# Plain float32 products for the first six head pairs of an attention and feed-forward kernel, with earlier weight loads and a fourth bank for scores

## The chip, the core and the metric

The kernel runs on one core of a Trainium2 chip. The core has a matrix engine (TensorE, PE in the profile; PEld is its loading of weights), three engines for elementwise work (VectorE or DVE, ScalarE or ACT, GpSimd or POOL) and an engine (SyncE or SP) that here issues every DMA. Each engine runs its own instructions in the order in which they were written and waits on semaphores for the others. Matrix products land in PSUM, eight banks of 512 float32 columns on 128 partitions; POOL does not touch PSUM in this kernel. The metric is the device time of one execution, in microseconds (us), the median of several runs.

## The reference

```python
# q, k, v: 8 batches x 12 heads x 448 x 64
q_n, k_n = rmsnorm(q, g_q), rmsnorm(k, g_k)
scores = (1 / np.sqrt(64)) * (q_n @ k_n.transpose(0, 1, 3, 2))
attn = softmax(scores)                   # along the last axis
x = (attn @ v)                           # to (8 * 448) x 768
h = x @ w_in                             # 768 x 2048
y = (h * np.cos(h)) @ w_out              # 2048 x 768
```

The feed-forward weights come in as float64.

## The kernel before

**Split products.** TensorE multiplies operands of type float32r. To keep precision every operand is split in two: a high part (a cast to float32r) and a low part (the float32 value minus the high one). A product A B is then three matmuls: high-high, high-low and low-high; low-low is left out.

**Tiling.** Two heads make a pair; there are 48 pairs, six for each of eight batches. A pair has seven score tiles of 128 queries by 448 keys: tiles 0 to 2 of one head, 4 to 6 of the other, and tile 3, which holds 64 queries of each. Tiles j and j+4 use the upper and lower 64 rows of TensorE side by side. For a pair u:

- `prepare(u)` loads q and k once in rows (tile `sd`) for their norms and once transposed (`qd`, `kd`). ACT squares, DVE sums, POOL takes the power -1/2; the key's factors go through DRAM (`rk_d`) and come back as a row over all partitions (`rkb`). `k_norm` and `q_scale` on POOL apply the factors in place; `k_high`, `q_high` on ACT and `k_low`, `q_low` on POOL split the results into `khi`, `kl`, `qhi`, `ql`. `v_load` fetches each head's v, and `v_high`, `v_low` on POOL split it into `vs`, with high and low parts side by side.
- `attend(u)` computes the scores into PSUM tiles `S` (ring of three banks). `rowmin` on DVE scales a tile in place and takes its minimum, `expo` on ACT makes the exponentials `P` and their sums `sm`. Then come four chunks of keys. In each, seven transposes (`transp`, L411) bring `P` into the tile `PT`, of which there is only one (two banks); in chunk 1 an eighth transpose (L413) turns the sums. `pt_high` on ACT copies both heads' halves of `PT` to `hi` (L418), `pt_low` on DVE subtracts (`lo`, L426; in the last chunk into 64 rows of an earlier `hi`, L428), and `av` on PE multiplies by `vs` into the tile `O` (L438). High and low parts of v stand side by side in the weights, so that `O` has 128 rows, of which `x_half` (ACT, L448) and `x_sum` (DVE, L453) add upper and lower half.
- `x_norm` and `x_split` make the operand `xs` of the first feed-forward layer, split too.

**The first layer** of a batch (`multiply`) is 16 tiles, each of 18 matmuls (three parts of six) into the bank `ph`; it runs mixed with the next batch's attention. The last batch's layer and the whole second layer (L552 to L554) follow when attention is over.

**Weights.** A tile of `w_in` is loaded as 64-bit words (`raw`) and decoded to float32 by four DVE steps (L211, L213, L215, L219) and one on ACT, then split by ACT and POOL. The first three tiles are begun at once, the others at a time that `WAHEAD` sets in the plan. `w_out` is decoded in the same way from batch 2 on and stored to DRAM.

**What sets the order.** All parts are handed to a planner (`Plan`): each with an engine, a cost, a due time, what it reads and writes, and for DMAs a time to land. It runs a list schedule: whenever an engine is free in the plan, it gets the ready part with the earliest due time. Rings of buffers (`RING`) are part of the dependencies. The sequence that results is written out as each engine's program, so a changed cost or dependency can change the whole order. The plan's times are the planner's own and not measured.

Of the kernel before, what the change touches and what calls it, by code (L numbers as in the profile page):

```python
# [10 lines left out]
F32 = mybir.dt.float32  # L11
# [115 lines left out]
def tile_attention_moe(  # L127
# [14 lines left out]
    NP = NU // B  # L142
    NQT = 7
    NVC = 5
    NSP = 0
    NCC = 6
    NFC = w_in.shape[0]
    NOC = 6
# [160 lines left out]

    def k_norm(u):  # L310
        kd = pair[u]["kd"]
        nc.gpsimd.tensor_tensor(kd, kd, pair[u].pop("rkb"), ALU.mult)

    def k_high(u):
        nc.scalar.copy(tl(u, "khi", [128, S], F32R), pair[u]["kd"])
# [7 lines left out]

    def q_scale(u):
        qd = pair[u]["qd"]
        nc.gpsimd.tensor_scalar(qd, qd, gsc, 0.0, op0=ALU.mult, op1=ALU.add)

    def q_high(u):
        nc.scalar.copy(tl(u, "qhi", [128, 512], F32R), pair[u]["qd"])
# [5 lines left out]
    def v_load(u, hh):  # L335
        nc.sync.dma_start(tl(u, f"vd{hh}", [128, NVC, D], F32, "vd"), v[u, :, hh * NVC : hh * NVC + NVC])

    def v_high(u, hh):
        if hh == 0:
            tl(u, "vs", [128, 2 * NVC, 2, D], F32R)  # L340
        vs = pair[u]["vs"][:, hh * NVC : hh * NVC + NVC]
        nc.gpsimd.tensor_scalar(vs[:, :, 0, :], pair[u][f"vd{hh}"], 1.0, 0.0, op0=ALU.mult, op1=ALU.add)
# [2 lines left out]
        vs = pair[u]["vs"][:, hh * NVC : hh * NVC + NVC]  # L345
        nc.gpsimd.tensor_tensor(vs[:, :, 1, :], pair[u].pop(f"vd{hh}"), vs.bitcast(F32)[:, :, 0, :], ALU.subtract)

    def spare(u, t):
        return t == 3 and u < NSP


    def score(u, j):
        d = pair[u]
        ops = (("qhi", "khi"), ("ql", "khi"), ("qhi", "kl"))
        if j == 0:
            tl(u, "sm", [128, 4, NQT], F32)
        tiles = (3,) if j == 3 else (j, j + 4)
        for t in tiles:
            pool, tag = (ps_h, "ph") if spare(u, t) else (ps_s, "S")
            d["S", t] = pool.tile([128, 512], F32, tag=tag, name=f"S{u}_{t}")  # L360
        for n, (a, c) in enumerate(ops):
            for t in tiles:
                p0, p1 = (0, 128) if t == 3 else (0, 64) if t < 3 else (64, 128)
                nc.tensor.matmul(  # L364
                    d["S", t][:, :S], d[a][p0:p1, j * 128 : j * 128 + 128], d[c][p0:p1, :],
                    start=(n == 0), stop=(n == 2),
                )

    def rowmin(u, t):
# [44 lines left out]

    def pt_high(u, kc, hh):
        d = pair[u]
        hi = d["hi", kc, hh] = apool.tile([128, S], F32R, tag="hi", name=f"hi{u}_{kc}_{hh}", bufs=RING["hi"])
        nc.scalar.copy(hi, pt[:, hh * S : hh * S + S])  # L418
# [11 lines left out]
    def av(u, kc, hh):  # L430
        d = pair[u]
        if kc == 0 and hh == 0:
            d["O"] = ps_o.tile([128, 2, 512], F32, tag="O", name=f"O{u}")
        O = d["O"][:, hh, :S]
        ops = (((0, "hi", 0), (0, "lo", 0)), ((1, "hi", 1), (1, "lo", 1)), ((3, "lo", 2),), ((2, "hi", 3), (4, "hi", 2)))
        for n, (c, what, kb) in enumerate(ops[kc]):
            st = d["vs"][:, hh * NVC + c].rearrange("p a d -> p (a d)")
            nc.tensor.matmul(O, st, d.pop((what, kb, hh)), start=(kc + n == 0), stop=(kc + n == 4))  # L438

    xf = {}  # L440
    xs = {}

    def x_half(u, hh):
        O = pair[u]["O"]
        if hh == 0:
            xf[u] = xpool.tile([128, S], F32, tag=f"xf{u % NP}", name=f"xf{u}")
        a, c = (0, 64) if hh == 0 else (64, 0)
        nc.scalar.copy(xf[u][a : a + 64], O[c : c + 64, hh, :S])  # L448

    def x_sum(u, hh):  # L450
# [121 lines left out]
    ISS, LAND = 0.45, 5.0  # L572
    PER0, PER = 16.0, 19.0
    SPLIT = 50.0
    WAHEAD = 50.0
    KTURN = 1

    def base(u):
# [34 lines left out]
    def prepare(u):  # L613
        D0 = base(u)
        sd, r, kd, khi, qd, qhi = ([(n, u)] for n in ("sd", "r", "kd", "khi", "qd", "qhi"))
        add(SP, ISS, D0 - 45, st_load, u, w=sd, land=6.5)
        add(SP, ISS, D0 - 36, k_load, u, w=kd, land=LAND)
        add(SP, ISS, D0 - 30, q_load, u, w=qd, land=LAND)
        add(ACT, 0.95, D0 - 40, st_square, u, w=sd)
        add(DVE, 1.08, D0 - 38, st_reduce, u, r=sd, w=r)  # L620
        add(DVE, 0.25, D0 - 37, st_mean, u, w=r)
        rq = [("rq", u)]
        if u:
            add(POOL, 2.6, D0 - 34, st_pow, u, 0, 14, w=r + rq)
        else:
            add(POOL, 1.5, D0 - 34, st_pow, u, 7, 14, w=r)
        add(SP, ISS, D0 - 30, st_store, u, r=r, w=[("rkd", u)], land=LAND if u else 3.6)
        add(SP, 2 * ISS, D0 - 26, rk_load, u, r=[("rkd", u)], w=[("rkb", u)], land=6.5 if u else 4.5)
        if not u:
            add(POOL, 1.5, D0 - 17, st_pow, u, 0, 7, r=r, w=rq)  # L630
        add(POOL, 1.22, D0 - 18, k_norm, u, r=[("rkb", u)], w=kd)
        add(ACT, 0.53, D0 - 14, k_high, u, r=kd, w=khi)
        add(POOL, 1.22, D0 - 12, k_low, u, r=kd + khi, w=[("kl", u)])
        add(DVE, 0.25, D0 - 10, st_negate, u, r=r + rq, w=[("nr", u)])
        add(POOL, 0.8, D0 - 16, q_scale, u, r=[("gsc", 0)] + ([] if u else r), w=qd)
        add(ACT, 0.6, D0 - 10, q_high, u, r=qd, w=qhi)
        add(POOL, 1.33, D0 - 8, q_low, u, r=qd + qhi, w=[("ql", u)])
        for hh in range(2):
            vd, vs = [("vd", 2 * u + hh)], [("vs", u, hh)]
            add(SP, ISS, D0 - 12 + 6 * hh, v_load, u, hh, w=vd, land=LAND)  # L640
            add(POOL, 0.56, D0 + 6 * hh, v_high, u, hh, r=vd + ([] if u else r), w=vs)
            add(POOL, 0.91, D0 + 2 + 6 * hh, v_low, u, hh, r=vd, w=vs)

    def attend(u):
# [3 lines left out]
        lead = 0.0 if u < NP else None  # L648
        for j in range(4):
            tiles = (3,) if j == 3 else (j, j + 4)  # L650
            keys = [("ph", u) if spare(u, t) else ("S", 7 * u + 2 * j + n - min(u, NSP)) for n, t in enumerate(tiles)]
            dj = D0 + step * j
            add(PE, 0.88 if j < 3 else 0.62, dj, score, u, j, lead=lead,
                r=[("qhi", u), ("ql", u), ("khi", u), ("kl", u)], w=keys)
            for t, key in zip(tiles, keys):
                add(DVE, 0.7, dj + 1, rowmin, u, t, r=[("nr", u)], w=[key, ("sm", u, 1, t)])
            for n, (t, key) in enumerate(zip(tiles, keys)):
                add(ACT, 0.94, dj + 2, expo, u, t, r=[key, ("sm", u, 1, t)],
                    w=[("P", 7 * u + 2 * j + n), ("sm", u, 2, t)])
# [156 lines left out]
```

## Time and profile before

| what | value |
|---|---|
| median of three runs, device time | 1561.55 us (1559.03 to 1561.74) |
| the profiled execution | 1562.97 us |
| its span, first to last instruction | 1560.9 us |
| mean granted TensorE clock | 0.986 of full |
| PE busy | 1468.3 us, 94%, 7680 matmuls |
| DVE busy | 1060.8 us, 68% |
| ACT busy | 884.4 us, 57% |
| POOL busy | 885.1 us, 57% |
| first score matmul | 24.09 us |
| last copy of `O` (`x_half` of pair 47) | begins at 1011.87 us |

A whole-span average mixes stages with different limits: the first batch's attention without any feed-forward work beside it, seven batches of attention with the first layer of the batch before mixed in, and the second layer alone. Read the profile by stages therefore. PE's busy time counts from the start of a matmul to its end, and matmuls overlap, so a busy PE may still be able to take more.

The page's second part shows the stages. Each digit is the busy share of a fortieth of the span (39 us) in tenths:

```profile
PE   2777998899999999999999999999999999999999
DVE  6677999877877777777776675432566566666561
PEclk9898999999999999999999999999999999999999
```

In the first four digits PE is not full, in the fifth to seventh DVE is at 9, then PE is.

### The profile page before, as it was taken

How to read it: one execution, taken by the hardware profiler on the slowest of the kernel's cores; microseconds unless marked ns; L12 is line 12 of the kernel's file. 1: busy time of each engine (PE TensorE's matmuls, PEld its weight loads, DVE VectorE, ACT ScalarE, POOL GpSimd, SP SyncE). 2: the span in 40 equal slices, each digit the busy share in tenths (PEclk: the TensorE clock that was granted, in tenths of full speed). 3: DMA queues.
4: the chain of work that ended last, by engine and by line, in shares of the span. 5: the costliest groups of instructions: out<-in, count | busy, mean ns of one | idle time of the engine just before them, and what ended most of it. 6: DMA issues, size and time to landing. Idle time of an engine off the chain costs nothing.

```text
span 1560.9 us, 22589 instructions
## 1 busy us (share of the span) xinstructions
PE 1468.3 (94%) x7680; PEld 1239.3 (79%) x7680; DVE 1060.8 (68%) x1915; ACT 884.4 (57%) x1786; POOL 885.1 (57%) x727
## 2 busy tenths in 40 slices
PE   2777998899999999999999999999999999999999
PEld 1544787788877788878787788889999999999998
DVE  6677999877877777777776675432566566666561
ACT  4675776777766766766676665442344344344341
POOL 7666788876766676675576463141454445444441
PEclk9898999999999999999999999999999999999999
DMA  5336653465555455545544432168133232232220
GB/s 169 115 105 200 199 164 96 123 191 179 178 154 157 144 174 160 160 144 153 162 135 148 127 126 72 48 234 307 48 94 97 69 95 95 71 95 95 71 71 36
DMA packets 118435, 205.26 MB, mean 131 GB/s; under 512 B 19680, under 2 KB 97840, under 8 KB 118320
## 3 DMA queue, kind: packets, MB, share of 16 engines
q1 hardware_dynamic: 118320, 203.82, 41.7%
q8 instruction: 60, 0.98, 0.3%
q14 instruction: 55, 0.45, 0.1%
HBM read 150.47 MB, written 53.30 MB: 131 GB/s over the span
## 4 chain that ended last, share of the span: by engine, by line
PE 73%; DVE 8%; ACT 2%; issue 2%; POOL 1%; DMA 1%; SPq 0%; ACTq 0%; POOLq 0%; DVEq 0%
PE y L554 10%; PE y L552 10%; PE y L553 10%; PE ph L481 8%; PE ph L482 7%; PE ph L483 7%; PE O L438 7%; PE PT L411 6%; PE S L364 6%; DVE lo L426 2%; ACT hi L418 1%; DVE S L371 1%; DVE xf L453 1%; DVE hi L428 1%; DVE wo L213 1%
## 5 line engine op out<-in xcount | busy, mean ns | idle before, releaser
L481 PE MATMUL ph<-xs,wi 128*128 128x448 f32 x768 | 299.7, 390 | 3.7 <-ACT he L493 3.5
L482 PE MATMUL ph<-xs,wi 128*128 128x448 f32 x768 | 283.3, 369 | 1.4 <-POOL xs L467 1.4
L483 PE MATMUL ph<-xs,wi 128*128 128x448 f32 x768 | 282.8, 368 | 1.5 <-POOL wi L234 1.5
L552 PE MATMUL y<-g,wo 128*128 128x448 f32 x768 | 282.1, 367 | 0.0
L553 PE MATMUL y<-g,wo 128*128 128x448 f32 x768 | 281.9, 367 | 0.0
L554 PE MATMUL y<-g,wo 128*128 128x448 f32 x768 | 281.9, 367 | 0.0
L384 ACT ACTIVATE P<-S,sm 128x448 f32<-128x448 f32 x336 | 214.2, 641 | 97.9 <-DVE S L371 87.1
L418 ACT CAST hi<-PT 128x448 fp32r<-128x448 f32 x384 | 188.6, 535 | 118.6 <-PE PT L411 57.9
L536 POOL TENSOR_TENSOR g<-r,g 128x896 fp32r<-128x896 f32 x64 | 139.9, 2186 | 189.5 <-ACT g L538 189.5
L371 DVE TENSOR_SCALAR_CACHE_REDUCE S<-S,nr 128x448 f32<-128x448 f32 x336 | 219.9, 683 | 30.4 <-PE S L364 26.0
L426 DVE TENSOR_TENSOR lo<-PT,hi 128x448 fp32r<-128x448 f32 x288 | 166.7, 617 | 91.2 <-ACT hi L418 90.4
L411 PE MATMUL PT<-ident,P 128*128 128x128 f32 x1344 | 186.9, 281 | 1.6 <-ACT P L384 1.6
L411 PEld LDWEIGHTS PT<-ident,P 128*128 128x128 f32 x1344 | 164.7, 145 | 18.5 <-issue 2.7
L481 PEld LDWEIGHTS ph<-xs,wi 128*128 128x128 f32 x768 | 145.3, 189 | 34.2 <-issue 11.8
L483 PEld LDWEIGHTS ph<-xs,wi 128*128 128x128 f32 x768 | 145.2, 189 | 14.7 <-POOL wi L234 1.8
L482 PEld LDWEIGHTS ph<-xs,wi 128*128 128x128 f32 x768 | 145.7, 190 | 12.7 <-POOL xs L467 3.3
L552 PEld LDWEIGHTS y<-g,wo 128*128 128x128 f32 x768 | 144.2, 188 | 13.8 <-ACT ye L562 0.2
L553 PEld LDWEIGHTS y<-g,wo 128*128 128x128 f32 x768 | 144.2, 188 | 13.3
L554 PEld LDWEIGHTS y<-g,wo 128*128 128x128 f32 x768 | 144.2, 188 | 13.3
L518 DVE TENSOR_TENSOR r<-hb,n 128x896 f32<-128x896 f32 x64 | 93.1, 1455 | 85.7 <-POOL g L536 81.8
L438 PE MATMUL O<-hi,vs 128*128 128x448 f32 x384 | 133.0, 395 | 18.3 <-DVE xf L453 10.2
L529 DVE TENSOR_TENSOR r<-r,hb 128x896 f32<-128x896 f32 x64 | 73.9, 1154 | 108.5 <-ACT r L525 108.5
(69 smaller groups left out, 2567.2 us busy)
## 6 DMA issues: line engine op xcount, KB each, us to landing
h_d<-he SPq DMA_DIRECT2D x128, 224.0 KB
hb<-h_d SPq DMA_DIRECT2D x64, 448.0 KB
sd<-sd SPq DMA_DIRECT2D x48, 448.0 KB
vd<-v SPq DMA_DIRECT2D x96, 160.0 KB
qd<-qT SPq DMA_DIRECT2D x48, 256.0 KB
raw<-w_in SPq DMA_DIRECT2D x16, 768.0 KB
rawo<-w_out SPq DMA_DIRECT2D x32, 384.0 KB
wo_d<-rawo SPq DMA_DIRECT2D x32, 384.0 KB
```

Source lines behind the costliest of these rows:

```text
L371: nc.vector.tensor_scalar(d["S", t][:, :S], d["S", t][:, :S], d["nr"][:, t : t + 1], None, op0=ALU.mult, op1=ALU.min, accum_out=d["sm"][:, ...
L384: nc.scalar.activation(tl(u, f"P{t}", [128, S], F32, "P"), d.pop(("S", t))[:, :S], AF.Exp, bias=sm[:, 1, t : t + 1], scale=-1.0, accum_out ...
L411: nc.tensor.transpose(pt[:, t * 128 : t * 128 + 128], src, ident)
L418: nc.scalar.copy(hi, pt[:, hh * S : hh * S + S])
L426: nc.vector.tensor_tensor(lo, src, hi.bitcast(F32), ALU.subtract)
L438: nc.tensor.matmul(O, st, d.pop((what, kb, hh)), start=(kc + n == 0), stop=(kc + n == 4))
L481: nc.tensor.matmul(ph[:, :S], whi, x2[:, 0, :], start=(cc == 0), stop=False)
L482: nc.tensor.matmul(ph[:, :S], whi, x2[:, 1, :], start=False, stop=False)
L483: nc.tensor.matmul(ph[:, :S], wlo, x2[:, 0, :], start=False, stop=(cc == NCC - 1))
L552: nc.tensor.matmul(y, whi, hi, start=(fc == 0), stop=False)
L553: nc.tensor.matmul(y, whi, lo, start=False, stop=False)
L554: nc.tensor.matmul(y, wlo, hi, start=False, stop=(fc == NFC - 1))
```

## The change

For the first six pairs (batch 0, `NS32` and `NA32` are 6) scores and P v are computed with plain float32 operands and one matmul where three split ones stood:

- `k_norm` and `q_scale` write their results straight into `khi` and `qhi`, as float32; the casts and the low parts of q and k go.
- `v_whole` loads both heads' v with one DMA straight into `vs`; the split of v goes. SP then waits for `vs` to be free (P v of the pair two before), where it waited for POOL.
- `pt_high` copies `PT` as float32, the first head's half on ACT and the second's on DVE; `pt_low` goes. `av` is one matmul per chunk and head into 64 rows of `O`, and `x_sum` goes.
- `place` gives every fourth score tile of these pairs the bank `ph`, ahead of its first use by the first layer.
- `WAHEAD` goes from 50 to 100, which lets the loads of weights 3 and up start earlier in the plan.

```diff
     def k_norm(u):
         kd = pair[u]["kd"]
-        nc.gpsimd.tensor_tensor(kd, kd, pair[u].pop("rkb"), ALU.mult)
+        k = tl(u, "khi", [128, S], F32) if u < NS32 else kd
+        nc.gpsimd.tensor_tensor(k, kd, pair[u].pop("rkb"), ALU.mult)
...
+    def v_whole(u):
+        t = tl(u, "vs", [128, 2, 2 * NVC, D], F32)
+        nc.sync.dma_start(t[:, 0], v[u])
...
+    def place(u, n):
+        i = 7 * min(u, NP) + (n if u < NP else 0)
+        if u < NP:
+            return ("ph", i // 4) if i % 4 == 3 else ("S", 3 * (i // 4) + i % 4)
+        return ("S", i - i // 4 + 7 * (u - NP) + n)
...
     def score(u, j):
-        ops = (("qhi", "khi"), ("ql", "khi"), ("qhi", "kl"))
+        ops = (("qhi", "khi"), ("ql", "khi"), ("qhi", "kl"))[: 1 if u < NS32 else 3]
...
     def pt_high(u, kc, hh):
+        dt = F32 if u < NA32 else F32R
...
+        if u < NA32 and hh == 1:
+            nc.vector.tensor_copy(hi, pt[:, hh * S : hh * S + S])
+        else:
+            nc.scalar.copy(hi, pt[:, hh * S : hh * S + S])
...
     def av(u, kc, hh):
+        if u < NA32:
+            rows, c = ((128, 0), (128, 1), (128, 3), (64, 2))[kc]
+            st = d["vs"][:rows, 0, hh * NVC + c]
+            nc.tensor.matmul(O[:D], st, d.pop(("hi", kc, hh))[:rows], start=(kc == 0), stop=(kc == 3))
+            return
...
     def x_half(u, hh):
         a, c = (0, 64) if hh == 0 else (64, 0)
+        if u < NA32:
+            c = 0
...
-    WAHEAD = 50.0
+    WAHEAD = 100.0
...
-            add(PE, 0.88 if j < 3 else 0.62, dj, score, u, j, lead=lead,
-                r=[("qhi", u), ("ql", u), ("khi", u), ("kl", u)], w=keys)
+            cost = (1.1 if j < 3 else 0.82) if u < NS32 else (0.88 if j < 3 else 0.62)
+            operands = ("qhi", "khi") if u < NS32 else ("qhi", "ql", "khi", "kl")
+            add(PE, cost, dj, score, u, j, lead=lead, r=[(n, u) for n in operands], w=keys)
```

The rest of the diff are the planner's entries for the same steps. Since costs, dependencies and rings changed, the planner writes another order. Two places show it; in the names the digit behind a letter is the pair (`S3_1` is tile 1 of pair 3; `hi2_0_1` is chunk 0, second head, of pair 2), and the number at the end only counts buffers.

PE, first chunk of a pair in batch 0, from the products of P v to the first transpose of the next chunk. Before, for pair 1:

```order
L438 MATMUL O1_498<-hi1_0_0_480,vs1_236 128x448
L438 MATMUL O1_498<-lo1_0_0_486,vs1_236 128x448
L438 MATMUL O1_498<-hi1_0_1_483,vs1_236 128x448
L438 MATMUL O1_498<-lo1_0_1_494,vs1_236 128x448
L411 MATMUL PT_98<-ident_88,P01_324 128x128
```

After the change, for pair 2, with the score group that stands ahead:

```order
L378 MATMUL S3_1_531<-khi3_431,qhi3_330 128x448
L378 MATMUL S3_5_532<-khi3_431,qhi3_330 128x448
L456 MATMUL O2_546<-hi2_0_0_537,vs2_398 64x448
L456 MATMUL O2_546<-hi2_0_1_544,vs2_398 64x448
L425 MATMUL PT_98<-ident_88,P02_378 128x128
```

Four matmuls, two of which waited for DVE's subtraction, have become two that wait for a copy each.

DVE, around the last scores of pair 4, when pair 3's chunks run. Before:

```order
L371 TENSOR_SCALAR S4_2_917,sm4_800<-S4_2_917,nr4_438 128x448
L371 TENSOR_SCALAR S4_6_918,sm4_800<-S4_6_918,nr4_438 128x448
L371 TENSOR_SCALAR S4_3_946,sm4_800<-S4_3_946,nr4_438 128x448
L426 TENSOR_TENSOR lo3_2_0_958<-PT_98,hi3_2_0_950 128x448
L426 TENSOR_TENSOR lo3_2_1_966<-PT_98,hi3_2_1_954 128x448
L377 TENSOR_SCALAR nr7_981<-r7_902 128x7
L428 TENSOR_TENSOR hi3_2_0_950<-PT_98,hi3_3_0_984 64x448
L428 TENSOR_TENSOR hi3_2_1_954<-PT_98,hi3_3_1_995 64x448
```

After the change:

```order
L434 COPY hi3_0_1_687<-PT_98 128x448
L291 TENSOR_SCALAR r7_680<-r7_680 128x14
L212 TENSOR_SCALAR wf4_699<-raw4_593 128x768
L214 SCALAR_TENSOR_TENSOR wf4_699<-raw4_593,wf4_699 128x768
L385 TENSOR_SCALAR S4_2_693,sm4_632<-S4_2_693,nr4_411 128x448
L385 TENSOR_SCALAR S4_6_694,sm4_632<-S4_6_694,nr4_411 128x448
L409 COPY rt3_722<-PT_98 7x128
L434 COPY hi3_1_1_730<-PT_98 128x448
L385 TENSOR_SCALAR S4_3_717,sm4_632<-S4_3_717,nr4_411 128x448
L391 TENSOR_SCALAR nr7_739<-r7_680 128x7
L220 SCALAR_TENSOR_TENSOR wf3_613<-raw3_535,wf3_613 128x768
L216 SCALAR_TENSOR_TENSOR wf4_699<-raw4_593,wf4_699 128x768
```

The subtractions are gone, one copy of `PT` per chunk has come, and steps of the decoding of weights 3 and 4 (`wf3`, `wf4`) now stand between row minima and copies; before, the decoding of weight 3 began only in pair 5's chunks.

More of the change, by code (lines that the diff above doesn't have):

```diff
@@ L144, in tile_attention_moe @@
     NVC = 5
-    NSP = 0
+    NS32, NA32 = 6, 6
     NCC = 6
@@ L325, in q_scale @@
         qd = pair[u]["qd"]
-        nc.gpsimd.tensor_scalar(qd, qd, gsc, 0.0, op0=ALU.mult, op1=ALU.add)
+        q = tl(u, "qhi", [128, 512], F32) if u < NS32 else qd
+        nc.gpsimd.tensor_scalar(q, qd, gsc, 0.0, op0=ALU.mult, op1=ALU.add)
     def q_high(u):
@@ L346, in v_low @@
         nc.gpsimd.tensor_tensor(vs[:, :, 1, :], pair[u].pop(f"vd{hh}"), vs.bitcast(F32)[:, :, 0, :], ALU.subtract)
-    def spare(u, t):
-        return t == 3 and u < NSP
+    def place(u, n):
[3 more added lines that the diff above has]
+        return ("S", i - i // 4 + 7 * (u - NP) + n)
+    NSP = 7 * NP // 4
     def score(u, j):
         d = pair[u]
-        ops = (("qhi", "khi"), ("ql", "khi"), ("qhi", "kl"))
+        ops = (("qhi", "khi"), ("ql", "khi"), ("qhi", "kl"))[: 1 if u < NS32 else 3]
         if j == 0:
@@ L357, in score @@
         tiles = (3,) if j == 3 else (j, j + 4)
-        for t in tiles:
-            pool, tag = (ps_h, "ph") if spare(u, t) else (ps_s, "S")
+        for n, t in enumerate(tiles):
+            tag = place(u, 2 * j + n)[0]
+            pool = ps_h if tag == "ph" else ps_s
             d["S", t] = pool.tile([128, 512], F32, tag=tag, name=f"S{u}_{t}")
@@ L365, in score @@
                     d["S", t][:, :S], d[a][p0:p1, j * 128 : j * 128 + 128], d[c][p0:p1, :],
-                    start=(n == 0), stop=(n == 2),
+                    start=(n == 0), stop=(n == len(ops) - 1),
                 )
@@ L416, in pt_high @@
         d = pair[u]
-        hi = d["hi", kc, hh] = apool.tile([128, S], F32R, tag="hi", name=f"hi{u}_{kc}_{hh}", bufs=RING["hi"])
-        nc.scalar.copy(hi, pt[:, hh * S : hh * S + S])
+        dt = F32 if u < NA32 else F32R
+        hi = d["hi", kc, hh] = apool.tile([128, S], dt, tag="hi", name=f"hi{u}_{kc}_{hh}", bufs=RING["hi"])
+        if u < NA32 and hh == 1:
+            nc.vector.tensor_copy(hi, pt[:, hh * S : hh * S + S])
+        else:
+            nc.scalar.copy(hi, pt[:, hh * S : hh * S + S])
     def pt_low(u, kc, hh):
@@ L630, in prepare @@
             add(POOL, 1.5, D0 - 17, st_pow, u, 0, 7, r=r, w=rq)
-        add(POOL, 1.22, D0 - 18, k_norm, u, r=[("rkb", u)], w=kd)
-        add(ACT, 0.53, D0 - 14, k_high, u, r=kd, w=khi)
-        add(POOL, 1.22, D0 - 12, k_low, u, r=kd + khi, w=[("kl", u)])
-        add(DVE, 0.25, D0 - 10, st_negate, u, r=r + rq, w=[("nr", u)])
-        add(POOL, 0.8, D0 - 16, q_scale, u, r=[("gsc", 0)] + ([] if u else r), w=qd)
-        add(ACT, 0.6, D0 - 10, q_high, u, r=qd, w=qhi)
-        add(POOL, 1.33, D0 - 8, q_low, u, r=qd + qhi, w=[("ql", u)])
+        if u < NS32:
+            add(POOL, 1.22, D0 - 18, k_norm, u, r=[("rkb", u)] + kd, w=khi)
+        else:
+            add(POOL, 1.22, D0 - 18, k_norm, u, r=[("rkb", u)], w=kd)
+            add(ACT, 0.53, D0 - 14, k_high, u, r=kd, w=khi)
+            add(POOL, 1.22, D0 - 12, k_low, u, r=kd + khi, w=[("kl", u)])
+        add(DVE, 0.25, D0 - 10, st_negate, u, r=r + rq, w=[("nr", u)])
+        if u < NS32:
+            add(POOL, 0.8, D0 - 16, q_scale, u, r=[("gsc", 0)] + qd + ([] if u else r), w=qhi)
+        else:
+            add(POOL, 0.8, D0 - 16, q_scale, u, r=[("gsc", 0)] + ([] if u else r), w=qd)
+            add(ACT, 0.6, D0 - 10, q_high, u, r=qd, w=qhi)
+            add(POOL, 1.33, D0 - 8, q_low, u, r=qd + qhi, w=[("ql", u)])
+        if u < NA32:
+            add(SP, ISS, D0 - 6, v_whole, u, w=[("vs", u, 0)], land=LAND)
+            return
         for hh in range(2):
@@ L650, in attend @@
             tiles = (3,) if j == 3 else (j, j + 4)
-            keys = [("ph", u) if spare(u, t) else ("S", 7 * u + 2 * j + n - min(u, NSP)) for n, t in enumerate(tiles)]
+            keys = [place(u, 2 * j + n) for n in range(len(tiles))]
             dj = D0 + step * j
-            add(PE, 0.88 if j < 3 else 0.62, dj, score, u, j, lead=lead,
-                r=[("qhi", u), ("ql", u), ("khi", u), ("kl", u)], w=keys)
+            cost = (1.1 if j < 3 else 0.82) if u < NS32 else (0.88 if j < 3 else 0.62)
+            operands = ("qhi", "khi") if u < NS32 else ("qhi", "ql", "khi", "kl")
+            add(PE, cost, dj, score, u, j, lead=lead, r=[(n, u) for n in operands], w=keys)
             for t, key in zip(tiles, keys):
@@ L679, in attend @@
                 n = 8 * u + 2 * kc + hh
-                add(ACT, 0.53, dk + 1, pt_high, u, kc, hh, r=[("pt", 0, hh)], w=[("hi", n)])
+                eng, cost = (DVE, 0.62) if u < NA32 and hh else (ACT, 0.53)
+                add(eng, cost, dk + 1, pt_high, u, kc, hh, r=[("pt", 0, hh)], w=[("hi", n)])
+                if u < NA32:
+                    continue
                 m = 6 * u + 2 * kc + hh
@@ L687, in attend @@
                 n, m = 8 * u + 2 * kc + hh, 6 * u + 2 * kc + hh
+                if u < NA32:
+                    add(PE, 0.82, dk + 4, av, u, kc, hh, lead=lead, r=[("vs", u, 0), ("hi", n)], w=[("O", u, hh)])
+                    continue
                 r = [[("hi", n), ("lo", m)], [("hi", n), ("lo", m)], [("lo", m)], [("hi", n), ("hi", n - 2)]][kc]
@@ L693, in attend @@
             add(ACT, 0.53, D2, x_half, u, hh, r=[("O", u, hh)], w=[("xf", u, hh)])
-            add(DVE, 0.62, D2 + 1, x_sum, u, hh, r=[("O", u, hh)], w=[("xf", u, hh)])
+            if u >= NA32:
+                add(DVE, 0.62, D2 + 1, x_sum, u, hh, r=[("O", u, hh)], w=[("xf", u, hh)])
         x = [("xf", u, 0), ("xf", u, 1)]
```

## The prediction

> **What bounds the kernel now.** I read the busy time by stretches first. Its columns are the stretch, its length, then busy us and instruction count of PE, PEld, DVE, ACT and POOL, the granted TensorE clock, the DMA share and GB/s.
>
> ```profile
> 43.25:137.59 94.34, 71.01 (x339) 48.36 (x338) 64.29 (x156) 60.37 (x142) 65.50 (x61) 0.89 0.42 124
> 137.59:160.63 23.04, 17.09 (x66) 11.54 (x64) 18.38 (x37) 14.32 (x31) 14.14 (x13) 0.71 0.52 177
> 160.63:330.83 170.20, 157.19 (x855) 128.26 (x854) 154.03 (x290) 122.55 (x267) 137.98 (x115) 0.97 0.50 154
> 330.83:1000.71 669.88, 656.34 (x3692) 540.08 (x3690) 490.58 (x1095) 454.85 (x1060) 400.75 (x375) 1.00 0.47 145
> 1100.00:1500.00 400.00, 400.00 (x1948) 365.16 (x1947) 251.38 (x236) 161.07 (x180) 189.96 (x108) 1.00 0.27 83
> ```
>
> The cuts lie at marks that occur once per pair, the transposition of the exponentials' sums (L413). They were taken from the timeline:
>
> ```profile
> 43.25 0.42 PE L413 MATMUL PT<-ident,sm 128*7 128x128 f32 x1
> 137.59 0.27 PE L413 MATMUL PT<-ident,sm 128*7 128x128 f32 x1
> 160.63 0.38 PE L413 MATMUL PT<-ident,sm 128*7 128x128 f32 x1
> 330.83 0.27 PE L413 MATMUL PT<-ident,sm 128*7 128x128 f32 x1
> 1000.71 0.27 PE L413 MATMUL PT<-ident,sm 128*7 128x128 f32 x1
> ```
>
> These are pairs 0, 5, 6, 14 and 47. Pairs 1 to 5 take 94.3/5 = 18.9 us each with no engine full. Pairs 7 to 14 take 21.3 us each with PE at 92% and DVE at 91%: in that stretch DVE decodes most of the 16 input weights. Pairs 15 to 47 take 20.3 us each with PE at 98%, and the output stage is PE without a gap. So only the time up to pair 14 can change much. Behind it the order of PE's instructions has the same number of first-layer matmuls between any two pairs as before, within 12 matmuls, so I take that part as unchanged.
>
> The last row gives the price of a split product: 400/1948 = 0.205 us from one 448-column matmul to the next (one record alone reads 0.37 us since neighbours overlap).
>
> What holds a pair at 18.9 us is seen in one of its four key chunks (timeline, pair 2 into pair 3):
>
> ```profile
> 76.57 0.93 PE L411 MATMUL PT<-ident,P 128*128 128x128 f32 x7
> 77.86 0.97 ACT L418 CAST hi<-PT 128x448 fp32r<-128x448 f32 x2
> 79.16 1.15 DVE L426 TENSOR_TENSOR lo<-PT,hi 128x448 fp32r<-128x448 f32 x2
> 79.27 0.44 PE L438 MATMUL O<-hi,vs 128*128 128x448 f32 x1 [1.78 <-DVE xf L453]
> 79.84 0.47 PE L438 MATMUL O<-lo,vs 128*128 128x448 f32 x1
> 81.57 0.92 PE L411 MATMUL PT<-ident,P 128*128 128x128 f32 x7
> ```
>
> Transposes, two ACT copies one behind the other, then two DVE subtractions, and only then may the one PT buffer be filled again: 81.57 - 76.57 = 5.0 us, of which PE computes under 2. The waits of pairs 1 to 5 (waiter, releaser, us in total, times, longest) say the same:
>
> ```profile
> PEld O L438 <- DVE lo L426: 15.7, 19, 1.9
> PEld O L438 <- ACT hi L418: 10.4, 11, 2.0
> ```
>
> **The change part by part, pairs 1 to 5.** The groups of that stretch (count, then busy us and mean ns):
>
> ```profile
> L418 ACT CAST hi<-PT 128x448 fp32r<-128x448 f32 x40 | 19.6, 535 | 17.4 <-PE PT L413 7.2 <-PE PT L411 5.1 <-DVE rt L395 2.3
> L426 DVE TENSOR_TENSOR lo<-PT,hi 128x448 fp32r<-128x448 f32 x30 | 17.5, 616 | 4.9 <-ACT hi L418 4.7
> L428 DVE TENSOR_TENSOR hi<-PT,hi 64x448 fp32r<-64x448 f32 x10 | 5.7, 611 | 9.0 <-ACT hi L418 9.0
> L453 DVE TENSOR_TENSOR xf<-O,xf 64x448 f32<-64x448 f32 x10 | 6.2, 622 | 2.0 <-ACT xf L448 1.8
> L346 POOL TENSOR_TENSOR vs<-vd,vs 128x320 fp32r<-128x320 f32 x10 | 8.6, 861 | 0.8
> ```
>
> Per pair DVE loses six L426, two L428 and two L453, 6.2 us, and gains four copies out of PT. No row shows such a copy; it reads what L426 reads less one operand, so I take 0.6 us, 2.4 in all (0.5 and 0.7 would change it by 0.4). ACT loses four of eight copies of 0.535 us, POOL the v splits and the low parts. These three had slack; what counts is the chain. The second copy no longer stands behind the first and no subtraction follows.
>
> PE gets more to do. A score group of two 64-row tiles now is six split products; the timeline shows it from 219.44 to 220.25, 0.81 us, or 0.27 for two products side by side:
>
> ```profile
> 219.44 0.47 PE L364 MATMUL S<-khi,qhi 64*128 64x448 f32 x2
> 220.25 0.47 PE L481 MATMUL ph<-xs,wi 128*128 128x448 f32 x1
> 217.23 0.93 PE L411 MATMUL PT<-ident,P 128*128 128x128 f32 x7
> 218.00 0.27 PE L413 MATMUL PT<-ident,sm 128*7 128x128 f32 x1
> ```
>
> The trace has no plain float32 product of 448 columns. Below, one costs 0.205 us as a split one; above, 4 x 0.205 = 0.82, all four products of high and low halves, of which the old code makes three. The only plain float32 operands here are the transposes, seven in 218.00 - 217.23 = 0.77 us, or 0.11 us for 128 columns; by columns 448 would cost 0.39. A transpose only moves data, so I take the upper end, 0.82, and 4 x 0.27 = 1.08 for two tiles side by side. At 0.39 a chunk (below) would be 0.86 us shorter, 17 us over five pairs. The Trainium skill, "FP8 and Floating Point Precision", section TensorE Precision Notes, counts four passes through the array for a true float32 product, which speaks against the change, as three split products do for it; by that page the price is 0.82 and the sum below stands, and no run here shows it yet.
>
> Per pair PE then has four transposition groups of 0.77, 3.1 us; scores 3 x 1.08 + 0.82 = 4.1; eight products for P v, 6.6: 13.7 us, up from 3.1 + 3 x 0.81 + 3 x 0.205 + 14 x 0.205 = 9.0. That is below 18.9, so it is hidden as long as the chain leaves room. The new chunk: transposes 0.93; 0.36 to the first copy (77.50 to 77.86); the copies beside each other, 0.54; 0.6 for the one instruction that such a copy finds ahead of it in its queue (a row minimum; the order also puts decode steps there); two products 1.64. Together 4.07 us, and the next score group (1.08) falls into the 1.5 us of waiting. Four make 16.3; with the clock at about 0.95 of full, between 0.89 and 0.97 of the rows with PE less and more busy, 16.5. **Five pairs: 5 x (16.5 - 18.9) = -12.** Bounds: 13.7 x 5 = 68.5, -26, or with the product at 0.39 -12 - 17 = -29 (at 0.205, which I count as out of reach, -37); no gain from the chain, 0.
>
> **Up to pair 0's mark.** The first scores now show these gaps:
>
> ```profile
> 23.47 0.56 ACT L315 CAST khi<-kd 128x448 fp32r<-128x448 f32 x1 [0.80 <-POOL kd L312]
> 25.70 0.74 PE L364 MATMUL S<-kl,qhi 64*128 64x448 f32 x2 [0.50 <-POOL kl L319]
> 29.20 0.74 PE L364 MATMUL S<-khi,qhi 64*128 64x448 f32 x1 [2.38 <-ACT P L384]
> 31.92 0.74 PE L364 MATMUL S<-khi,qhi 64*128 64x448 f32 x1 [1.24 <-ACT P L384]
> ```
>
> The cast of k (0.56) goes, since POOL writes that operand itself; so does the wait for the low part (0.50); the 2.38 us wait for one of three banks goes with the fourth. Together **-3.5**. The second wait for a bank, 1.24, may go too, -4.7; or the third weight's decode on DVE, which stands ahead of the last row minima, takes it all, 0.
>
> **Pair 5 to pair 6**, now 23.0 us: three plain chunks at 4.1 and one split at 5.0, 17.3, less certain as decodes are denser: **-5**, bounds 0 and -7.
>
> **Pair 6 to pair 14.** Decode steps move. Their means between pairs 6 and 10:
>
> ```profile
> L219 DVE SCALAR_TENSOR_TENSOR wf<-raw,wf 128x768 f32<-128x768 f32 x7 | 8.5, 1211 | 0.0
> L215 DVE SCALAR_TENSOR_TENSOR wf<-raw,wf 128x768 int32<-128x768 int32 x7 | 7.8, 1116 | 0.0
> L213 DVE SCALAR_TENSOR_TENSOR wf<-raw,wf 128x768 int32<-128x768 int32 x6 | 7.4, 1238 | 0.0
> L211 DVE TENSOR_SCALAR wf<-raw 128x768 int32<-128x768 int32 x6 | 5.1, 858 | 0.0
> ```
>
> One decode is 4.4 us. By the order 3.25 decodes stand before pair 5's mark now and 6.75 after the change; in pairs 1 to 5 DVE has 64.3 - 5 x 3.8 + 3.5 x 4.4 = 61 us in 82, so it hides them. Between the marks of pairs 6 and 14 stand 11.25 decodes (those of the output weights among them) where 13.5 stood, -9.9 us; other work that slides in is 4.8 us by the same count. DVE is 91% busy there, so 5.1/0.91: **-6**. Bounds: 0 if PE (157 of 170 us) takes over at once, -11 for the decodes alone (9.9/0.91).
>
> **SP's queue.** The v loads waited for POOL:
>
> ```profile
> SPq L336 <- POOL vs L346: 21.7, 8, 4.8
> ```
>
> One whole load per pair replaces two. It waits for PE's last product of the pair two before, and behind it on SP stand the next k, rk and sums transfers. That product lies most of a pair earlier, so I cost this at nothing; if a load is issued 4.8 us early, the prepared pair behind it is late by as much, inside the bound of 0 above. The fourth bank is the first layer's: its first tile starts behind the last score tile of pair 5 in it, which costs PE nothing before pair 5, where 12 of 18 matmuls of that tile were all it could do.
>
> Sum: -3.5 - 12 - 5 - 6 = -26.5. The profiled execution took 1562.97 us (span 1560.9), so 1536.5; the median of the runs is 1.4 us lower, so **1535**.
>
> **The rivals.**
> - The queues take the chain's place: decode steps of 1.1 us, not one row minimum, stand ahead of DVE's copies, as the order shows in pairs 3 to 5, and a chunk takes 4.6 us. Then 18.4 per pair, -2.5, with -2, -2 and -4 for the rest: -10.5, so 1551. For it: DVE is in order. Against: DVE has 61 us of work in over 90.
> - PE runs without pauses: 14.6 us per pair (PE's 13.7 and one wait of 0.9), -21, with -5, -6 and -10: -42, so 1520; a product at 0.39 gives the same, -43. For it: a score group is at hand in nearly every chunk. Against: the order also shows chunks with none.
> - Slower, by the clock: plain products fill PE, and it is granted half the clock, as seven transposes in 1.70 us instead of 0.93 hint (row below). At half, 27.4 us per pair, +42, other terms near 0: 1604. It decides from 21.6 us per pair, where five pairs eat the other 13.5 us; with 2.8 us of waiting that is 18.8 of PE for 13.7, a mean clock of 0.73. Against: the stretches give more clock where PE is busier, 0.89 at 75% and 1.00 at 98%. The Trainium skill, "TensorE: Matmul & The Clock Gate", Part 1, has the gate opened by sustained activity; by that rule, and those rows agree, this rival falls and the time stays at the forecast's.
> - It is given back: pairs run ahead, but pairs 6 to 14 wait for weights just as long, as PE is near full there; with the queues' rival, within 0.2% of 1561.
>
> ```profile
> 66.54 1.70 PE L411 MATMUL PT<-ident,P 128*128 128x128 f32 x7
> ```
>
> **How the numbers follow.** My forecast 0.58, queues 0.20, no pauses 0.12, half clock 0.07, given back 0.03. About 0.2%, 3 us, is what a measurement can tell from no change: faster 0.90, same 0.03, slower 0.07. The range from 1518 to 1553 takes in the forecast's bounds and the two neighbours and leaves some 0.18 out.
>
> **What would show it.** Right: marks of pairs 1 to 5 some 16.5 us apart; plain products 0.8 us apart; no wait for a low part; pair 6 at about 140 us, pair 14 at about 304; the rest as before. Wrong: a plain product over 1.25 us, a granted clock under 0.75 before 140 us, SP waiting for PE at the v load with pairs late behind it, or marks behind pair 14 that drift.

## The result, and the profile after

| | before | after |
|---|---|---|
| median | 1561.64 us (1559.03 to 1566.49, 4 runs) | 1521.57 us (1518.63 to 1522.58, 4 runs) |
| ratio, 95% interval | 1 | 0.9742 (0.9719 to 0.9764) |
| span of the profiled execution | 1560.9 us | 1520.0 us |
| mean granted TensorE clock | 0.986 | 0.999 |

The change makes the kernel 40 us faster. The forecast was 1535 (1518 to 1553): the side and the range were right, the gain was half as large again as the 26.5 us of its sum.

The marks are again the transposition of the sums (now L427) of pairs 0, 5, 6, 14 and 47, here from the timeline after the change:

```profile
40.46 0.27 PE L427 MATMUL PT<-ident,sm 128*7 128x128 f32 x1
120.08 0.27 PE L427 MATMUL PT<-ident,sm 128*7 128x128 f32 x1
135.20 0.27 PE L427 MATMUL PT<-ident,sm 128*7 128x128 f32 x1
301.80 0.27 PE L427 MATMUL PT<-ident,sm 128*7 128x128 f32 x1
963.81 0.27 PE L427 MATMUL PT<-ident,sm 128*7 128x128 f32 x1
```

Busy time by stretches after the change, with columns as before the change (stretch, length, PE, PEld, DVE, ACT, POOL, granted clock, DMA share, GB/s); the fourth cut, 238.61, is pair 11 and the sixth, 498.51, pair 24:

```profile
40.46:120.08 79.62, 75.89 (x318) 32.65 (x315) 62.20 (x143) 55.19 (x128) 56.11 (x42) 1.00 0.64 200
120.08:135.20 15.12, 13.95 (x69) 7.26 (x66) 14.21 (x33) 12.40 (x27) 13.88 (x12) 1.00 0.72 238
135.20:238.61 103.41, 95.55 (x533) 77.74 (x530) 96.81 (x181) 76.36 (x165) 85.08 (x71) 1.00 0.47 140
238.61:301.80 63.19, 60.30 (x339) 48.59 (x336) 52.67 (x114) 46.52 (x107) 50.21 (x43) 1.00 0.55 167
301.80:498.51 196.71, 196.05 (x1117) 163.35 (x1114) 146.25 (x334) 138.20 (x319) 120.70 (x115) 1.00 0.51 157
498.51:963.81 465.30, 455.75 (x2566) 375.25 (x2564) 338.10 (x743) 310.48 (x728) 270.30 (x257) 1.00 0.44 137
```

Pairs 1 to 5 now take 79.6 us, of which PE is busy 75.9, 95% where it was 75%, and the granted clock is 1.00 where it was 0.89. The cuts at the same pairs before the change:

```profile
160.63:263.42 102.79, 93.96 (x519) 76.22 (x518) 98.28 (x175) 72.96 (x158) 82.01 (x68) 0.98 0.51 160
263.42:330.83 67.41, 63.23 (x337) 52.04 (x336) 55.76 (x116) 49.59 (x109) 55.97 (x48) 0.95 0.49 146
330.83:537.54 206.71, 202.75 (x1140) 166.94 (x1138) 161.72 (x356) 146.23 (x336) 132.26 (x120) 1.00 0.54 165
537.54:1000.71 463.17, 453.60 (x2554) 373.13 (x2552) 328.86 (x739) 308.62 (x724) 268.49 (x256) 1.00 0.44 137
```

One chunk after the change (timeline, pair 0's third chunk with the last scores of pair 1):

```profile
43.27 0.98 PE L425 MATMUL PT<-ident,P 128*128 128x128 f32 x7
44.18 1.97 PE L378 MATMUL S<-khi,qhi 64*128 64x448 f32 x6
44.34 0.53 ACT L436 COPY hi<-PT 128x448 f32<-128x448 f32 x1 [0.16 <-PE PT L425]
45.84 0.62 DVE L434 COPY hi<-PT 128x448 f32<-128x448 f32 x1
46.08 1.72 PE L456 MATMUL O<-hi,vs 128*64 128x448 f32 x4
47.73 0.44 PE L425 MATMUL PT<-ident,P 128*128 128x128 f32 x2
```

PE has no pause in it: from 43.27 to 47.73 it transposes, computes scores, multiplies by v and transposes again. Each plain product shows as two records: the four of L456 are two products, (47.73 - 46.08)/2 = 0.82 us each, the price that the forecast took. The six of L378 are a side-by-side pair and a single tile, 46.08 - 44.18 = 1.90 us, and 1.08 + 0.82 were expected.

PE's waits in pairs 1 to 5 (waiter, releaser, us in total, times, longest), before and then after the change:

```profile
PE O L438 <- DVE lo L426: 8.3, 8, 1.4
PE O L438 <- DVE xf L453: 7.1, 5, 1.8
PE S L364 <- ACT P L384: 5.0, 3, 1.8
```

```profile
PE O L456 <- ACT hi L436: 2.1, 4, 0.6
PE O L456 <- DVE hi L434: 1.5, 4, 0.5
PE O L456 <- ACT xf L473: 0.2, 1, 0.2
```

What waited for subtractions, for the two halves of `O` to be added and for a bank is gone; 3.8 us are left.

By marks, the forecast and the measured difference:

| stretch | before | after | difference | forecast |
|---|---|---|---|---|
| to pair 0's mark | 43.3 | 40.5 | -2.8 | -3.5 |
| pairs 0 to 5 | 94.3 | 79.6 | -14.7 | -12 |
| 5 to 6 | 23.0 | 15.1 | -7.9 | -5 |
| 6 to 14 | 170.2 | 166.6 | -3.6 | -6 |
| 14 to 24 | 206.7 | 196.7 | -10.0 | 0 |
| 24 to 47 | 463.2 | 465.3 | +2.1 | 0 |
| behind 47 | 560.2 | 556.2 | -4.0 | 0 |

The last row is no effect of the change: in the fourteen profiled executions of this study that stretch, whose work is the same in all, lay between 553.7 and 560.2 us.

### The profile page after: what moved, and what is told of

Read it like the earlier page. It is cut to its first block, busy times and chain, and to the rows that moved or that the text cites. A ratio compares the mean times of both kernels' runs of the same rounds, so it can differ in the third digit from the quotient of the medians.

```text
span 1520.0 us, 22367 instructions
## 1 busy us (share of the span) xinstructions
PE 1462.9 (96%) x7650; PEld 1213.4 (80%) x7650; DVE 1042.9 (69%) x1879; ACT 866.9 (57%) x1750; POOL 853.8 (56%) x691
## 4 chain that ended last, share of the span: by engine, by line
PE 84%; DVE 8%; ACT 3%; issue 2%; POOL 2%; DMA 1%; SPq 0%; ACTq 0%; DVEq 0%; POOLq 0%
PE y L577 10%; PE y L578 10%; PE y L579 10%; PE ph L506 10%; PE ph L507 9%; PE ph L508 9%; PE PT L425 8%; PE O L461 8%; PE S L378 8%; PE O L456 2%; DVE lo L444 1%; ACT hi L436 1%; DVE S L385 1%; DVE xf L478 1%; POOL xs L492 1%
## 5 line engine op out<-in xcount | busy, mean ns | idle before, releaser
L436 ACT CAST hi<-PT 128x448 fp32r<-128x448 f32 x336 | 165.0, 536 | 84.7 <-PE PT L425 42.9
L444 DVE TENSOR_TENSOR lo<-PT,hi 128x448 fp32r<-128x448 f32 x252 | 145.5, 617 | 76.2 <-ACT hi L436 75.6
L425 PEld LDWEIGHTS PT<-ident,P 128*128 128x128 f32 x1344 | 157.3, 141 | 33.5 <-issue 20.7
L425 PE MATMUL PT<-ident,P 128*128 128x128 f32 x1344 | 181.8, 275 | 1.0 <-ACT P L398 1.0
L295 POOL TENSOR_TENSOR r<-r,nhalf 128x14 f32<-128x14 f32 (+1 forms) x49 | 127.1, 2595 | 40.0 <-DVE r L291 35.9
```

The costliest lines, as they stand in the source:

```text
L425: nc.tensor.transpose(pt[:, t * 128 : t * 128 + 128], src, ident)
L444: nc.vector.tensor_tensor(lo, src, hi.bitcast(F32), ALU.subtract)
```

## The experiments

Each kernel is compared with before by the ratio of medians; marks come from one profiled execution each. Theory 1 is that batch 0 was limited by the chain transposes, copies, P v; theory 2 that the earlier weights carry the gain.

**E1, plain products alone.** In the changed kernel:

```diff
     def place(u, n):
-        i = 7 * min(u, NP) + (n if u < NP else 0)
-        if u < NP:
-            return ("ph", i // 4) if i % 4 == 3 else ("S", 3 * (i // 4) + i % 4)
-        return ("S", i - i // 4 + 7 * (u - NP) + n)
-
-    NSP = 7 * NP // 4
+        return ("S", 7 * u + n)
+
+    NSP = 0
...
-    WAHEAD = 100.0
+    WAHEAD = 50.0
```

> The changed kernel with WAHEAD back at 50 and no fourth bank: plain products alone. Theory 1 (the chain from transposes to copies to P v was the limit of batch 0): pairs 1 to 5 keep most of the changed kernel's pace, 80 to 84 us from mark to mark instead of 94.3, pair 6's mark stands near 140 us, and the whole is 22 to 30 us under before. Theory 2 (the earlier weights carry the gain): pair 6's mark may come early, but pairs 6 to 14 give most of it back while they wait for decodes, over 178 us from mark 6 to mark 14 instead of 170 and 167, and the whole is at most 12 us under before.

Measured: 1537.79 us, ratio 0.9859 (0.9837 to 0.988), 22 us under before. Pairs 1 to 5 take 76.9 us, pair 6's mark stands at 139.7, and 6 to 14 takes 172.3: theory 1. Theory 2 falls as it stands, but 18 of the 40 us are missing.

**E2, late weights.** In the changed kernel:

```diff
-    WAHEAD = 100.0
+    WAHEAD = 50.0
```

> The changed kernel with WAHEAD back at 50, fourth bank kept. Theory 1: 5 to 10 us slower than the changed kernel, lost between the marks of pairs 6 and 24, where decodes of input weights fill DVE again; pairs 1 to 5 a little faster than the 79.6 us of the changed kernel, since no decode steps stand between row minima and copies. Theory 2: 25 us or more slower than the changed kernel.

Measured: 1531.75 us (0.9818, 0.9792 to 0.9843), 10 us slower than the changed kernel, as theory 1 had it. Pairs 1 to 5 are faster, 74.7 us, and what is lost is behind pair 6: 173.5 from 6 to 14 and 207.1 from 14 to 24.

**E3, earlier weights alone.** In the kernel before:

```diff
-    WAHEAD = 50.0
+    WAHEAD = 100.0
```

> Before with WAHEAD at 100 and nothing else. Theory 1: pairs 1 to 5 stay at 94 us or get slower by some us as decode steps lengthen the same chain, and what is gained between pairs 6 and 24 is 5 to 10 us: the whole is 0 to 8 us under before. Theory 2: 20 us or more under before.

Measured: 1552.59 us (0.9954, 0.9938 to 0.9971), 7.4 us under before. Two stretches of it, pairs 1 to 5 and pairs 7 to 14:

```profile
43.69:144.10 100.41, 75.80 (x334) 53.10 (x332) 76.13 (x164) 64.44 (x147) 75.31 (x65) 0.82 0.56 177
166.29:325.99 159.70, 153.06 (x862) 125.64 (x860) 143.66 (x285) 121.81 (x268) 123.78 (x108) 1.00 0.43 131
```

Pairs 1 to 5 get 6 us longer. More of DVE's decode steps (5.75 decodes ahead of pair 5's mark, 3.25 before) stand beside the old chain there, and the granted clock is 0.82 for 0.89; which of the two costs the time was not separated. From 6 to 14 10.5 us are won. So the two parts help each other: products alone give 22, weights alone 7, and both without the fourth bank (E4) 39.

**E4, three banks.** The changed kernel with `place` and `NSP` as in E1.

> The changed kernel without the fourth bank. Theory 1 as forecast: some 3 us later at pair 0's mark and little else, the whole 2 to 5 us slower than the changed kernel. Rival: with three banks the score groups come late in every chunk of pairs 1 to 5, 1 us per pair or more, and the whole is 8 us or more slower.

Measured: 1520.85 us (0.9746, 0.9723 to 0.9769), the same as the changed kernel, with pair 0's mark at 40.64. Neither expectation came: with early weights the fourth bank brings nothing. With late ones it is 1537.79 (E1) against 1531.75 (E2), 6 us. Mark 6 comes 10 us earlier with the bank, over half of it between pairs 5 and 6 (15.8 against 21.2), and 4 us are lost again behind it; I did not follow this up.

**E5, plain P v alone,** and **E6, plain scores alone.** In the changed kernel, E5 and E6:

```diff
-    NS32, NA32 = 6, 6
+    NS32, NA32 = 0, 6
```

```diff
-    NS32, NA32 = 6, 6
+    NS32, NA32 = 6, 0
```

> The changed kernel with split scores (NS32 = 0): only P v is plain. Theory 1 (the chain transposes, copies, P v is what became shorter): pairs 1 to 5 stay within 5 us of the changed kernel's 79.6 us, the whole within 8 us of it. Rival (POOL's load from splitting q and k was the limit): pairs 1 to 5 go back to 90 us or more and the whole is 12 us or more slower than the changed kernel.

> The changed kernel with split P v (NA32 = 0): only the scores are plain. Theory 1: the chain is the old one, pairs 1 to 5 take 92 to 100 us as with the earlier weights alone (100.4), and the whole stays within 6 us of that run's 1552.6. Rival: pairs 1 to 5 under 88 us and the whole under 1540.

Measured: E5 1527.8 us (0.9791, 0.9773 to 0.9809), E6 1541.95 us (0.9895, 0.9875 to 0.9914). Pairs 1 to 5 of each, E5 first:

```profile
44.18:124.60 80.42, 73.23 (x351) 36.12 (x348) 60.78 (x137) 55.98 (x129) 56.21 (x43) 1.00 0.63 194
```

```profile
40.99:135.00 94.01, 72.88 (x308) 44.00 (x305) 76.39 (x167) 61.86 (x144) 57.82 (x52) 0.85 0.57 176
```

P v alone gives the new pace, 80.4 us; scores alone leave the old one, 94.0, and PE at 78%. So the chain is what went. E5 also drops POOL's split of v, but PE's waits before the change name subtractions, the sum of the halves and banks, and none names `vs`. But E6 as a whole is 10.6 us under E3, where I expected 6 at most: pair 6's mark is 12 us earlier than in E3 (154.5 against 166.3), 2.7 of them before pair 0's mark. Against E3, which has the same weights, pairs 1 to 5 are 6 us shorter too. Plain scores do take work off a stretch in which the earlier decodes stand; POOL's busy time there falls from 75.3 to 57.8 us, but no run shows that this is what counts.

**E7, a busier PE.** In the kernel before:

```diff
         for t in tiles:
             src = pair[u][f"P{t}"][:, KS[kc] : KS[kc] + 128]
             nc.tensor.transpose(pt[:, t * 128 : t * 128 + 128], src, ident)
+        if u < 3 and tiles[0] == 4:
+            if "t" not in idle:
+                idle["t"] = ps_h.tile([128, 512], F32, tag="ph", name="idle")
+            w = wts[("wi", 0)][:, 0]
+            for _ in range(6):
+                nc.tensor.matmul(idle["t"][:, :S], w[:, :128], w[:, 128 : 128 + S], start=True, stop=True)
```

> Before with six more split products behind the transposes of every chunk of pairs 0 to 2, into a bank that is free then; nobody reads them, and the order of all else is as before. They take 1.2 us of PE per chunk in which it waits for the copies. If the granted clock costs batch 0 time: the clock in pairs 1 to 2 rises from 0.8 to 0.9 towards 1.00 and the marks of pairs 0 to 3 come 2 us or more closer (57.9 us before). If only the chain counts: the clock rises and the marks stay within 1 us, or come 1 to 3 us later because P v stands behind the new products. The whole moves by no more than 4 us either way.

Measured: 1565.36 us (1.0041, 1.0026 to 1.0056). From pair 0 to pair 3 (45.18 to about 108.3) it takes 63 us, 5 more than before; the granted clock rose from 0.85 only to 0.92. Both expectations missed: the marks came later by more than 3 us, and the whole is some 6 us over before, not 4 at most. More PE work did not pay for itself by the clock, but the six products stood ahead of others in the chain, so what the clock alone is worth stays open.

**E8, still earlier weights.** In the changed kernel:

```diff
-    WAHEAD = 100.0
+    WAHEAD = 150.0
```

> The changed kernel with WAHEAD at 150, so that still more decodes fall into batch 0. Theory 1 (earlier decodes cost batch 0 about 1 us each on DVE and give 2 us each back behind pair 6): pairs 1 to 5 take 82 to 86 us, the stretch from mark 6 to mark 24 is 4 to 8 us shorter than the changed kernel's 363, and the whole is 0 to 4 us faster. Rival (DVE is full in batch 0 by now): pairs 1 to 5 over 88 us and the whole 3 us or more slower.

Measured: 1533.87 us (0.9839, 0.982 to 0.9858), 12 us slower than the changed kernel. Pairs 1 to 5 take 86.7 and 5 to 6 19.9 us, and behind pair 6 nothing is won beyond the changed kernel. The rival holds as to the time: batch 0 does not hide more decodes. Its reason is not shown, as DVE is busy for 71.4 of the 86.7 us and so not full.

**E9, both copies on ACT.** In the changed kernel, with the same change in the plan's entry:

```diff
-        if u < NA32 and hh == 1:
+        if False:
             nc.vector.tensor_copy(hi, pt[:, hh * S : hh * S + S])
```

> The changed kernel with both copies out of PT on ACT, one behind the other, as before; no subtraction follows. If the copies beside each other are what shortens a chunk (a step of the forecast): 0.5 us or more per chunk comes back, pairs 1 to 5 take 88 us or more instead of 79.6, and the whole is 8 us or more slower than the changed kernel. If DVE's queue is what a chunk waits for: DVE has 2.4 us less per pair, pairs 1 to 5 take 75 to 81 us, and the whole is the same or up to 5 us faster.

Measured: 1523.8 us (0.9765, 0.9732 to 0.9798). Pairs 1 to 5:

```profile
39.20:114.40 75.20, 72.89 (x312) 32.11 (x309) 48.02 (x116) 59.10 (x143) 42.38 (x34) 1.00 0.61 190
```

They got faster, not slower, with the copies one behind the other. Part of it is that this plan puts 5.0 decodes ahead of pair 5's mark and not 6.75; E11, with 4.75, took 77.0. E12 below, with both copies on ACT and three banks, has 6.75 again and takes 79.6, as the changed kernel does. So copies beside each other are not what shortened the chunk.

**E10, some products twice.** In the changed kernel:

```diff
-            nc.tensor.matmul(O[:D], st, d.pop(("hi", kc, hh))[:rows], start=(kc == 0), stop=(kc == 3))
+            hi = d.pop(("hi", kc, hh))[:rows]
+            if kc == 0:
+                nc.tensor.matmul(O[:D], st, hi, start=True, stop=True)
+            nc.tensor.matmul(O[:D], st, hi, start=(kc == 0), stop=(kc == 3))
```

> The changed kernel with the plain products of the first chunk of each of the six pairs done twice over, the second writing over the first; the order of all else is as it was. That is 2 x 0.78 = 1.6 us more PE per pair. If PE is the limit of batch 0 now: marks of pairs 0 to 5 spread by 6 to 9 us, and the whole is 6 to 10 us slower than the changed kernel. If the chain through ACT and DVE still is: under 3 us in both.

Measured: 1529.64 us (0.9805, 0.978 to 0.9829), 8 us slower than the changed kernel. Pairs 1 to 5:

```profile
42.83:129.27 86.44, 83.22 (x338) 35.49 (x335) 63.14 (x143) 55.27 (x128) 56.05 (x41) 1.00 0.59 186
```

6.8 us more, for five times 1.6 = 8 us of added PE, as expected if PE is the limit of batch 0 now. By itself this does not settle it: the added products stand between the copies and the next transposes, so a chain with waits in it would also grow by them. That PE is the limit rests on its busy time, 75.9 of 79.6 us, and on the 3.8 us of waits. The order of all else is that of the changed kernel, and so are the later stretches: 165.8, 196.7 and 464.9 us against 166.6, 196.7 and 465.3. In these two executions the same order gave the same times to within 0.8 us.

**E11, weights between,** and **E12, E9 with three banks.** In the changed kernel, E11, and E12 with the edits of E9 and E4:

```diff
-    WAHEAD = 100.0
+    WAHEAD = 75.0
```

> The changed kernel with WAHEAD at 75, between the late weights (1531.75) and 100 (1521.57). If the time falls evenly with the number of decodes in batch 0 up to where DVE is full: 1525 to 1528, pairs 1 to 5 near 77 us, marks 6 to 24 near 371 us. If 100 already puts too many decodes ahead of copies: under 1520.

> The changed kernel with both copies out of PT on ACT and without the fourth bank. Earlier runs: copies on ACT alone took 4.4 us off pairs 1 to 5 and lost it behind pair 6; three banks alone lost nothing. If both hold together: pairs 1 to 5 at 75 to 77 us, marks 6 to 47 at 827 to 830 us, the whole 1515 to 1519, faster than the changed kernel. If the planner's order behind pair 6 decides: marks 6 to 47 at 833 us or more and the whole between 1520 and 1526.

Measured: E11 1531.14 us (0.9816, 0.9791 to 0.9841), no better than late weights; pair 6's mark stands at 139.1, 4 us later than with 100, and my even fall did not come. E12 1525.19 us (0.9776, 0.9742 to 0.9811): pairs 1 to 5 took 79.6, and 6 to 47 831.8, so the two gains did not add up. No kernel of the study is clearly faster than the changed one; E4 does as well with a bank less.

All kernels together, in us of one profiled execution each:

| weights | kernel | to mark 6 | mark 6 to mark 47 |
|---|---|---|---|
| 50 | before, E7 | 160.6, 170.8 | 840.1, 840.5 |
| 50 | E1, E2 | 139.7, 129.7 | 840.0, 843.9 |
| 75 | E11 | 139.1 | 837.2 |
| 100 | E3, E6 | 166.3, 154.5 | 830.0, 827.9 |
| 100 | changed, E4, E5 | 135.2, 135.7, 139.6 | 828.6, 826.5, 831.1 |
| 100 | E9, E10, E12 | 130.4, 144.4, 136.6 | 835.3, 827.4, 831.8 |
| 150 | E8 | 148.4 | 829.1 |

The time behind mark 6 goes with the weights. The time to mark 6 is set mostly by the products (31 us from E3 to the changed kernel); the weights move it by 4 us (E1 to E4, earlier) to 13 us (changed to E8, later).

## Why the forecast was right, and where it was too small

- **What bounded batch 0** (the chain, not an engine): shown. E5 takes the subtractions and the sum of the two halves out and has the new pace; E6 leaves them and has the old one. How much of the 14.7 us is waits and how much is the clock, which rose from 0.89 to 1.00 as the waits went, stays open. An estimate of the most that the clock can be: if all 71.0 us of PE's busy time had lain on the chain and had run at 1.00, 0.11 x 71.0 = 7.8 us.
- **The price of a plain product**: 0.82 us, and 1.08 for two side by side, as taken. By the Trainium skill, "FP8 and Floating Point Precision", section TensorE Precision Notes, a true float32 product is four passes; the trace agrees with 0.82 against 0.205.
- **The chunk of 4.07 us**: the size was near (79.6/20 = 3.98), in part by luck. I had transposes, a wait of 1.5 us and two products, with scores inside the wait. What the chunk above and PE's waits show is PE almost without a pause, so the row "PE runs without pauses" of the rivals is what came in this stretch, at 15.9 us per pair and not 14.6, as PE's own work is more than my 13.7 (75.9/5 = 15.2 by its busy time). By the starts of the records, less the waits, a pair's transposes take 3.7 us and not 3.1, the products of P v 6.9 and not 6.6, the scores 4.1 as forecast, and 12 matmuls of the first layer, which the 13.7 left out, 0.6. So a chain with a wait in it and PE's own work, counted too short, met at nearly the same size. The clock's part of the sum was wrong as well: at 0.95 the 2.57 us of transposes and products in a chunk give 0.5 us more per pair, where the sum has 0.2, so its own terms make some -10 and not -12. Measured, the clock was 1.00. The step that copies beside each other save half a microsecond fell in E9 and E12: with both copies on ACT the stretch is no longer.
- **To pair 0's mark**: -2.8 for -3.5, but not in the forecast's way. Without the fourth bank (E4) the mark is at 40.64 all the same. The first scores begin at 21.72 us where they began at 24.09, which is 2.4 of the 2.8 us; for that the sum had only the cast, 0.56. The waits for a bank, 3.6 us before, are 1.1 us in E4 with three banks.
- **DVE hides the decodes in batch 0**: nearly. DVE's busy time in pairs 1 to 5 came as forecast, 62.2 us for 61. The forecast set the cost of the decodes there at nothing; late weights (E2) are 5 us faster from pair 0 to 5 than the changed kernel, and at 150 (E8) another 7 us are lost.
- **SP's wait for v** costs little: 3.5 us in three waits up to pair 6, the longest 1.7, where the waits for POOL's split of v had been 25.3 up to that mark:

```profile
SPq L343 <- PE O L456: 3.5, 3, 1.7
```

- **Half the clock** is out: 1.00 was granted in pairs 1 to 5.
- **"The time can change only up to pair 14"**: this step failed. Some of the row 14 to 24 is no gain: 23 fewer matmuls than before fall between these marks (1117 for 1140), 14 more between 6 and 14 (869 in the row below, 855 before) and 12 more between 24 and 47. At 0.205 us each that moves 4.7, 2.9 and 2.5 us, so that, with equal matmuls, an estimate of the differences is -6.5, -5.3 and -0.4 us:

```profile
135.20:301.80 166.60, 155.84 (x869) 126.33 (x866) 149.48 (x294) 122.89 (x272) 135.29 (x113) 1.00 0.50 150
```

The -6 up to pair 14 was then near, and some 5 us behind it were missed. The forecast took the 4.8 us of other work that slides into pairs 6 to 14 on DVE off the gain, but did not count that this work is then missing behind pair 14. Its sum for DVE up to pair 14 was near: 149.5 us for 154.0, -4.5 where the sum has -5.1. But from 14 to 24, where it has nothing, DVE works 146.3 us for 161.7. From mark 6 to mark 14 stand 7.75 decodes of input weights where 11.5 stood, and 3.5 of output weights where 2 stood; from 14 to 24 stand 9.5 of output weights where 11 stood. Norm reductions slide in the same way. In the ten pairs from mark 14 to 24, before and after the change:

```profile
L286 DVE TENSOR_REDUCE r<-sd 128x14 f32<-128x896 f32 x14 | 15.1, 1081 | 0.2
```

```profile
L287 DVE TENSOR_REDUCE r<-sd 128x14 f32<-128x896 f32 x10 | 10.9, 1086 | 0.3
```

Before, fourteen were done for ten pairs; after, four of those were done ahead of mark 14, three of them from mark 6 on (11 where 8 stood). That such work is put off does not itself cost the time: E4 has fourteen reductions from 14 to 24 as well, gains 10.8 us from mark 6 to 14 and 6.1 from 14 to 24, and is as fast from mark 6 to 47 (826.5 us). It shifts the gain between the two stretches. So the term of the weights has to be taken over the whole way: from mark 6 to mark 47 it is 828.6 - 840.1 = -11.5 us for the -6 of the sum. The experiments show that the weights do it: with `WAHEAD` at 50 that time is 840 to 844 us whatever the products do, at 75 it is 837, at 100 or 150 it is 826 to 835. That they act through DVE's work was read from these counts and not tried by itself.

## What to carry to other kernels

A trick that saves an engine's work can cost more than it saves where that engine waits: three split products were cheaper on PE than one plain product, but the copies and subtractions around them held a stage of PE at 75%. Spend idle time of one engine to shorten the chain, then put other work (here decodes) into the time that the chain's engines gain; each alone gave 22 and 7 us, together 39. And when work is moved out of a stretch, other work slides in: it is then missing further on. Sum the effect over the whole way on which work can move, and compare stretches only at equal counts of the limiting engine's instructions.

## What the runs showed of the hardware

- A plain float32 product of 448 columns is two matmul records and takes 0.82 us of PE, against 0.205 us for a float32r product. In pairs 1 to 5 of the changed kernel the middle value is 0.43 us from record to record, with 64 or 128 rows of weights alike.
- The granted clock was lower where PE was less busy: in pairs 1 to 5 of the kernels 0.82 and 0.85 where PE was busy 75 and 78% (E3, E6), 0.89 at 75% (before), 0.98 at 88% (E8), 1.00 at 91% and above (E5, E9, E10, the changed kernel). E7 at 82% had 0.92 in its stretch. The share alone does not set it, as 0.82 and 0.89 at the same 75% show. How much of the gain is the clock's was not separated.
